# Two attention blocks, gated: projections as two 64-row sums in two PSUM banks, and the maxima shared out anew

## The chip, the cores and the metric

The kernel runs on one core of a Trainium2 chip. The engines of a core work side by side, each in the order of its own instruction list, and wait for each other by semaphores: TensorE (PE; its weight loads are shown as PEld), VectorE (DVE), ScalarE (ACT), GpSimd (POOL), and SyncE (SP), which here only issues DMAs. Matmul results go to PSUM, of which the kernel uses eight banks of 128 x 512 float32. The metric is the device time of one execution in microseconds (us), lower is better, as the median of several runs.

## The reference

Two multi-head attention blocks A and B with weights of their own work on the same input `x` (1 x 2048 x 640), with 32 heads of 20 features each. A gate per token mixes their outputs.

```python
g = _sigmoid((x * gate_w).sum(-1, keepdims=True))
qkv = (x @ wqkv).reshape(B, S, 3, H, Dh)          # H = 32, Dh = 20
scores = jnp.einsum("bhqd,bhkd->bhqk", q, k) * scale
p = _softmax(scores, axis=-1)
o = jnp.einsum("bhqk,bhkd->bhqd", p, v)
a = o.transpose(0, 2, 1, 3).reshape(B, S, D) @ wo     # b likewise
return g * a + (1 - g) * b
```

The softmax is over 2048 keys, for 2048 queries, 32 heads and two blocks. Everything is float32; the kernel holds operands of score and projection matmuls as sums of two float16 parts (`hi` and `lo`).

## The kernel before

**Groups and steps.** The work is cut into 16 groups `g` of four heads (eight per attention block), four query blocks `qb` of 512 queries, and eight steps `i` of 256 keys: 512 steps `G` in all. In each step TensorE makes eight score tiles of 128 keys x 512 queries (`scores`, L632; a head's features fill 64 of the array's 128 rows, so that two heads run at once in the upper and the lower half). ScalarE turns each into exponentials (L635). Two value products (`values`, L650: four heads side by side, 128 rows each, float32) add the step before's exponentials times V into the bank `acc`; a column of ones beside V collects the sum of the exponentials. Behind the last step of a query block `take_acc` divides, on VectorE and GpSimd, and stores.

**Maxima.** The softmax's maximum is found ahead of time, by units that run some 15 steps before the step that needs them. One unit (`max_mm`, L574) makes eight score tiles of 128 queries x 512 keys: four key chunks `ch`, taken in the order 0, 2, 1, 3, times two heads `j`. Each tile is reduced by VectorE to one maximum per query (L585). There is a second form, by key differences: as max(a, b) = b + max(a - b, 0), chunk 0 is multiplied with the difference of the keys of chunks 0 and 1 (tile `kd`), ScalarE takes the relu (L578), and VectorE adds chunk 1 to it and reduces both in one fused operation (L582, followed by a short read of its accumulator). So two reductions on VectorE become one relu on ScalarE and one fused operation. Before the change this is done for head `j == 0` of each pair, and for both heads in the first group.

**Projections.** Q, K and V of the coming group, the rest of Q, and the outputs `o @ wo` are made beside the steps, in blocks of 15 matmuls (9 or 6 for outputs over fewer features) that add up in one bank: five chunks of 128 features times the three products hi x hi, hi x lo, lo x hi. These matmuls use all 128 rows. `mms` (L375) issues them. `project_chunk` makes 512 tokens in three blocks of 176, 168 and 168 columns, and ScalarE copies each out of PSUM with a scale `QKS` (L402); GpSimd splits the chunk into two float16 parts (L404, L405). `project_v` makes 160 columns and ScalarE copies them into V (L530). `out_tiles` makes blocks of 160 or 320 columns; the first job is scaled out by ScalarE (L715), the others are scaled and added by VectorE (L717). The first group's projections run ahead of the steps, in another order, with 512 columns.

**Banks and order.** One of the eight PSUM banks is `acc`; seven are handed out by `take`, which picks the bank that is free earliest by the planner's own clock (`clock`, `free_at`, with costs such as `T_EXP`), and given back by `give` when its reader is through. The planner only chooses banks; the order of work in a step is written out by hand in `STEP`, one line for steps with no, one, or two blocks: `e0`/`e1` is a score tile of the upper or lower half, `m0`/`m1` a tile for the maxima, `V` a value product, and `X` a projection block.

```python
STEP = ("e0 m1 V e1 m0 e0 m1 e1 m0 e0 m1 e1 m0 V e0 m1 e1 m0",
        "X e0 m1 m0 e1 m0 m1 V m1 e0 e1 m0 e1 e0 V m0 e1 e0 m1",
        "X m0 m1 e0 m1 e0 e1 V e1 e0 m1 m0 V e1 m0 m1 m0 e0 e1 X")
```

So in a step with one block, X follows the four scores with which the step before ended, and six scores follow X before the first V. All engines run their lists strictly in this order.

**Queues.** Nearly all DMAs are issued by SP (`nc.sync`), one after the other: the spread of Q and K into the tiles that scores read (`spread`, `rows`, L421 and L423), the key differences (`spread_differences`), maxima, outputs.

Of the kernel before, what the change touches and what calls it, by code (L numbers as in the profile page):

```python
# [11 lines left out]
F32 = mybir.dt.float32  # L12
I32 = mybir.dt.int32
AF = mybir.ActivationFunctionType
# [47 lines left out]
def kernel(  # L62
# [18 lines left out]
    psum = ctx.enter_context(tc.tile_pool(name="psum", bufs=1, space=PSUM))  # L81
# [18 lines left out]
    acc = psum.tile([P, QB], F32, name="acc")  # L100
# [59 lines left out]
    def scales(maxima, n, then):  # L160
# [5 lines left out]
        nc.tensor.transpose(pt[:n, :P], maxima[:, :n], ident)  # L166
# [3 lines left out]
        nc.vector.tensor_reduce(e[:n, 0:1], pt[:n, :P], axis=AX.X, op=OP.max)  # L170
# [11 lines left out]
        for k in range(2):  # L182
            nc.tensor.matmul(pb[:, k * n:(k + 1) * n], ones[:n, :], dg[:n, k, :n], start=True, stop=True)  # L183
        yield
        both = wts.tile([P, 10], F32, name="both", tag="scb", bufs=2)
        nc.vector.tensor_copy(both[:, :2 * n], pb[:, :2 * n])
# [181 lines left out]
    def mms(i, out_ap, pairs, cost):  # L368

        if now[0] >= 0:  # L370
            tick_block(len(pairs) * cost * T_SCORE, free_at[i])
        for k, (a, b) in enumerate(pairs):
            if now[0] < 0:
                tick_block(cost * T_SCORE, free_at[i])
            nc.tensor.matmul(out_ap, a, b, start=(k == 0), stop=(k == len(pairs) - 1))  # L375
            if now[0] < 0:
                yield
# [6 lines left out]
    def project_chunk(w, hi, lo, ch):  # L384
# [9 lines left out]
        if now[0] >= 0:  # L394
            f = work.tile([P, QB], F32, name="fs")
            for k in range(3):
                if k:
                    yield
                m = slice(PARTS[k], PARTS[k + 1])
                i, pt = take()  # L400
                yield from mms(i, pt[:, m], pairs(slice(t0 + m.start, t0 + m.stop)), 0.34)
                nc.scalar.activation(f[:, m], pt[:, m], AF.Copy, scale=QKS)  # L402
                give(i, spend("act", 0.25, clock["done"]))
# [115 lines left out]
    def project_v(gg, j):  # L519
# [3 lines left out]
        for u in range(2):  # L523
            if u and now[0] >= 0:
                yield
            n = slice((j + u) * P, (j + u + 1) * P)
            i, pt = take()
            yield from mms(i, pt[:, :w], [(a[:, c, n], b[:, c, :w]) for c in range(NC) for a, b in
                                          ((xh, wh), (xh, wl), (xl, wh))], 0.33)
            nc.scalar.activation(V[gg % 2][:, j + u, :, 0:DH], pt[:, :160].rearrange("p (h d) -> p h d", h=2 * GH),  # L530
                                 AF.Copy, scale=QKS)
            give(i, spend("act", 0.25, clock["done"]))
            v_done.add((gg, j + u))
            if gg == 0:
                nc.scalar.activation(gates[:, 0, j + u:j + u + 1], pt[:, 160:161], AF.Exp, scale=inv_g)
# [16 lines left out]
    relus, relu_at = {}, {}  # L552

    def max_parts(g, qb):
        m = mparts[g, qb] = wts.tile([P, 2, 2, 4, 4], F32, name="mpart", tag="mpart", bufs=2)
        nc.gpsimd.memset(m[:, :, 0:1 if g else 2, :, 0] if g or qb else m, LOW)

    def max_mm(u, ch, heads=(0, 1)):
# [9 lines left out]
        for j in heads:  # L568
            two = u < NS or ch < 2 and (j == 0 or g == 0)
# [4 lines left out]
            nc.tensor.matmul(pt, QT[g % 2][r, pair, q0:q0 + P], k, start=True, stop=True)  # L574
            m = mparts[g, qb][:, pair, j, t, ch:ch + 1]
            if two and ch % 2 == 0:
                relus[u, j] = start.tile([P, QB], F32, name="rl0", bufs=4) if u < NS else work.tile([P, QB], F32, name="rl", bufs=2)
                nc.scalar.activation(relus[u, j], pt, AF.Relu)  # L578
                back = relu_at[u, j] = spend("act", T_EXP, ready)
            elif two:  # L580
                rl = relus.pop((u, j))
                nc.vector.tensor_tensor_reduce(rl, pt, rl, 1.0, LOW, OP.add, OP.max, m)  # L582
                back = spend("dve", T_MAX, max(ready, relu_at.pop((u, j))))
            else:
                nc.vector.tensor_reduce(m, pt, axis=AX.X, op=OP.max)  # L585
# [38 lines left out]
    def scores(G, kk, pair, heads=(0, 1)):  # L624
# [3 lines left out]
        for j in heads:  # L628
# [3 lines left out]
            nc.tensor.matmul(et, KT[g % 2][r, pair, kt * P:(kt + 1) * P],  # L632
                             QT[g % 2][r, pair, qb * QB:(qb + 1) * QB], start=True, stop=True)
            pt = pp.tile([P, QB], F32, name="pt")
            nc.scalar.activation(pt, et, AF.Exp, scale=factor(g // 4))  # L635
# [49 lines left out]
    def out_tiles(job, t, state):  # L685
# [491 lines left out]
```

## Time and profile before

| | us |
|---|---|
| median of 3 runs (2834.72 to 2834.99) | 2834.94 |
| span of the profiled execution | 2832.8 |
| TensorE busy | 2773.1 |
| ScalarE busy | 2529.7 |
| VectorE busy | 2443.8 |
| GpSimd busy | 671.8 |
| share of projections (L375) in the chain that ended last | 20% |

The profiled execution's span is 2.1 us under the median of the runs. In rows of instruction groups, the line of the kernel and the engine come first, then what is written and read, the shapes, and the count; behind the bar stand the group's busy time in us, the mean ns of one, and how long the engine stood idle before them, with what ended that. In a timeline a row has its start and length in us; neighbours of one kind are merged (x2, x6). A matmul's row is longer than the time it holds the array, since they are pipelined: the distance of two starts tells what one costs. The mean granted clock of TensorE was 0.996.

### The profile page before, as it was taken

How to read it: one execution, taken by the hardware profiler on the slowest of the kernel's cores; microseconds unless marked ns; L12 is line 12 of the kernel's file. 1: busy time of each engine (PE TensorE's matmuls, PEld its weight loads, DVE VectorE, ACT ScalarE, POOL GpSimd, SP SyncE). 2: the span in 40 equal slices, each digit the busy share in tenths (PEclk: the TensorE clock that was granted, in tenths of full speed). 3: DMA queues.
4: the chain of work that ended last, by engine and by line, in shares of the span. 5: the costliest groups of instructions: out<-in, count | busy, mean ns of one | idle time of the engine just before them, and what ended most of it. 6: DMA issues, size and time to landing. Idle time of an engine off the chain costs nothing.

```text
span 2832.8 us, 62443 instructions
## 1 busy us (share of the span) xinstructions
PE 2773.1 (98%) x23362; PEld 970.8 (34%) x23362; DVE 2443.8 (86%) x4763; ACT 2529.7 (89%) x5122; POOL 671.8 (24%) x914
## 2 busy tenths in 40 slices
PE   6999999999999999999999999999999999999998
PEld 3533223342323323343233333334333333332222
DVE  6688999879999898988989888887888989989982
ACT  3799999989999999989999999998899999888887
POOL 5312113231221212233431111222112233120011
PEclk9999999999999999999999999999999999999999
DMA  4110101001020101202021020211202112122222
GB/s 135 35 45 7 39 6 42 16 16 29 13 52 16 37 11 27 47 13 50 17 56 44 14 60 16 48 37 24 49 15 61 38 38 70 55 71 60 63 60 74
DMA packets 167170, 113.71 MB, mean 40 GB/s; under 512 B 102224, under 2 KB 140808, under 8 KB 166864
## 3 DMA queue, kind: packets, MB, share of 16 engines
q1 hardware_dynamic: 164320, 108.09, 15.6%
q8 instruction: 183, 3.00, 0.4%
q0 software_dynamic: 1600, 0.96, 0.2%
q14 instruction: 123, 1.01, 0.1%
q10 hardware_dynamic: 944, 0.66, 0.1%
HBM read 48.89 MB, written 26.61 MB: 27 GB/s over the span
## 4 chain that ended last, share of the span: by engine, by line
PE 91%; DVE 5%; ACT 1%; DMA 1%; POOL 1%; issue 1%; SPq 0%; POOLq 0%; DVEq 0%; ACTq 0%
PE acc L650 34%; PE bank L375 20%; PE bank L632 19%; PE bank L574 17%; DVE mpart L585 3%; ACT pt L635 1%; DVE rl L582 1%; DMA xs<-in_A_x_dram 0%; ACT rl L578 0%; DMA wv<-in_A_wqkv_dram 0%; DVE ot L736 0%; PE bank L813 0%; PE bank L183 0%; PE bank L862 0%; DVE wmax L227 0%
## 5 line engine op out<-in xcount | busy, mean ns | idle before, releaser
L635 ACT ACTIVATE pt<-bank 128x512 f32<-128x512 f32 x4096 | 2157.5, 614 | 155.0 <-PE bank L632 75.1
L585 DVE TENSOR_REDUCE mpart<-bank 128x1 f32<-128x512 f32 x2976 | 1867.8, 681 | 264.3 <-PE bank L574 167.1
L650 PE MATMUL acc<-pt,v 128*21 128x512 f32 x8192 | 1082.0, 600 | 3.4 <-DVE ot L736 3.1
L632 PE MATMUL bank<-qt,kt 64*128 64x512 f16 x4096 | 1056.3, 380 | 11.9 <-ACT pt L635 4.5
L574 PE MATMUL bank<-kt,qt 60*128 60x512 f16 x3536 | 1013.0, 380 | 4.0 <-DVE mpart L585 0.7
L574 PEld LDWEIGHTS <-qt 60*128 60x128 f16 x4096 | 235.4, 94 | 686.6 <-issue 629.0
L632 PEld LDWEIGHTS <-kt 64*128 64x128 f16 x4096 | 248.1, 94 | 456.7 <-issue 322.8
L582 DVE CUSTOM_DVE_ANT_0 rl<-bank,rl 128x512 f32<-128x512 f32 x560 | 377.5, 678 | 20.5 <-ACT rl L578 8.2
L578 ACT ACTIVATE rl<-bank 128x512 f32<-128x512 f32 x560 | 329.8, 595 | 14.6 <-PE bank L574 12.3
L744 POOL TENSOR_TENSOR ot<-ot,sq 128x512 f32<-128x512 f32 x63 | 66.0, 1047 | 993.0 <-DVE sq L741 993.0
L650 PEld LDWEIGHTS acc<-pt,v 128*21 128x21 f32 x8192 | 143.0, 99 | 434.6 <-issue 421.5
L375 PE MATMUL bank<-xx,wbh 128*128 128x168 f16 (+2 forms) x2240 | 280.1, 244 | 3.2 <-ACT xx L866 1.9
L375 PE MATMUL bank<-xx,wbl 128*128 128x168 f16 (+2 forms) x1120 | 252.8, 243 | 0.0
L375 PEld LDWEIGHTS <-wbh 128*128 128x128 f16 x2240 | 183.6, 98 | 86.8 <-issue 79.8
L574 PE MATMUL bank<-kd,qt 60*128 60x512 f16 x560 | 203.6, 381 | 1.7 <-DMA kd<-dd 1.2
L375 PE MATMUL bank<-wvh,xx 128*128 128x160 f16 (+1 forms) x1280 | 155.4, 234 | 0.5 <-ACT pt L635 0.3
L375 PE MATMUL bank<-woh,o_in 128*128 128x160 f16 (+1 forms) x960 | 155.7, 256 | 0.0
L375 PEld LDWEIGHTS <-xx 128*128 128x128 f16 x1920 | 131.6, 97 | 52.7 <-issue 49.4
L404 POOL CAST cq<-fs 128x512 f16<-128x512 f32 x60 | 36.6, 609 | 446.0 <-ACT fs L402 444.0
L375 PE MATMUL bank<-wvl,xx 128*128 128x160 f16 (+1 forms) x640 | 137.3, 231 | 0.6 <-POOL wvl L315 0.6
L375 PEld LDWEIGHTS <-o_in 128*128 128x128 f16 (+1 forms) x1440 | 104.0, 97 | 75.3 <-issue 62.2
L402 ACT ACTIVATE fs<-bank 128x168 f32<-128x168 f32 (+1 forms) x216 | 67.5, 313 | 56.6 <-PE bank L375 40.0
(131 smaller groups left out, 1305.2 us busy)
## 6 DMA issues: line engine op xcount, KB each, us to landing
y_scr<-y_out SPq DMA_DIRECT2D x32, 320.0 KB
kt<-cq SPq DMA_DIRECT2D x120, 80.0 KB
o_scr<-on SPq DMA_DIRECT2D x240, 40.0 KB
kt<-cq SPq DMA_DIRECT2D x136, 40.0 KB
xs<-in_A_x_dram SPq DMA_DIRECT2D x8, 640.0 KB
o_in<-o_scr SPq DMA_DIRECT2D x32, 160.0 KB
y_out<-y_scr SPq DMA_DIRECT2D x16, 320.0 KB
xx<-y_scr SPq DMA_DIRECT2D x16, 320.0 KB
```

The costliest lines, as they stand in the source:

```text
L375: nc.tensor.matmul(out_ap, a, b, start=(k == 0), stop=(k == len(pairs) - 1))
L402: nc.scalar.activation(f[:, m], pt[:, m], AF.Copy, scale=QKS)
L404: nc.gpsimd.tensor_copy(hi, f)
L574: nc.tensor.matmul(pt, QT[g % 2][r, pair, q0:q0 + P], k, start=True, stop=True)
L578: nc.scalar.activation(relus[u, j], pt, AF.Relu)
L582: nc.vector.tensor_tensor_reduce(rl, pt, rl, 1.0, LOW, OP.add, OP.max, m)
L585: nc.vector.tensor_reduce(m, pt, axis=AX.X, op=OP.max)
L632: nc.tensor.matmul(et, KT[g % 2][r, pair, kt * P:(kt + 1) * P], QT[g % 2][r, pair, qb * QB:(qb + 1) * QB], start=True, stop=True)
L635: nc.scalar.activation(pt, et, AF.Exp, scale=factor(g // 4))
L650: nc.tensor.matmul(acc[32 * h:32 * h + VW, :], V[(g // 2) % 2][:, kt, (g % 2) * GH + h, :], ptiles.pop((G, kk, h)), start=(kt == 0), stop= ...
L744: nc.gpsimd.tensor_tensor(t3, t3, sq.unsqueeze(2).to_broadcast([P, 16, 32]), op=OP.mult)
```

## The change

Three things are changed.

**The form of a projection block.** Each matmul over 128 rows becomes two over 64 rows each, which run at once in the two halves of the array, like scores. Each half adds up in a bank of its own; the two banks are neighbours, and one VectorE instruction (`tensor_reduce` over the two) adds them and writes the sum. ScalarE has no part in it any more. What it scaled is now scaled elsewhere: V isn't scaled (its ones become `1 / QKS`), chunks of Q and K are scaled on GpSimd before the split, and outputs are scaled and added on GpSimd. The projections ahead of the steps stay as they were. For the steps the seven banks are one tile (`store`), and `apart` lifts waits between readers and writers of different banks, over the last 24 readers; the last few instructions of the kernel (`alone=False`) keep theirs.

**The maxima.** In every second unit (`u % 2`) both heads use the key differences, instead of one head.

**What follows from that.** The key differences are spread for both heads in every group: four more DMAs on SP for each of 15 groups.

```diff
-    psum = ctx.enter_context(tc.tile_pool(name="psum", bufs=1, space=PSUM))
+    psum_acc = ctx.enter_context(tc.tile_pool(name="psum_acc", bufs=1, space=PSUM))
+    psum_start = ExitStack()
+    psum = psum_start.enter_context(tc.tile_pool(name="psum", bufs=1, space=PSUM))
...
-    acc = psum.tile([P, QB], F32, name="acc")
+    acc = psum_acc.tile([P, QB], F32, name="acc")
     banks = [psum.tile([P, QB], F32, name=f"bank{i}") for i in range(NB)]
...
+    def take_two():
+
+        i = min((k for k in range(NB - 1) if k not in held and k + 1 not in held),
+                key=lambda k: (max(max(free_at[k:k + 2]), clock["pe"]), abs(free_at[k] - free_at[k + 1])))
+        held.update((i, i + 1))
+        return (i, i + 1), store[0][:, i:i + 2]
+
+    store, last_read = [], {}
+
+    fresh, recent = set(), []
+
+    def apart(ins, keep):
+
+        for r, engine in recent:
+            if r not in keep and engine != ins.engine:
+                tc.declare_no_dep(ins, r, reason="a reader of another bank")
+
+    def on_bank(out, ins, alone=True):
+
+        if store:
+            i = out.offset // QB
+            if alone:
+                apart(ins.ins, last_read.get(i, []))
+            fresh.add(i)
+        return ins
+
+    def matmul(out, a, b, start=True, stop=True, alone=True):
+        return on_bank(out, nc.tensor.matmul(out, a, b, start=start, stop=stop), alone)
+
+    def transpose(out, a, alone=True):
+        return on_bank(out, nc.tensor.transpose(out, a, ident), alone)
+
+    def read(banks_read, ins, keep=(), alone=True):
+
+        name = ins.ins.name
+        if store:
+            for i in banks_read:
+                if i in fresh:
+                    fresh.discard(i)
+                    last_read[i] = []
+                last_read[i].append(name)
+            if alone:
+                apart(ins.ins, keep)
+            recent.append((name, ins.ins.engine))
+            del recent[:-24]
+        return name
...
     def mms(i, out_ap, pairs, cost):
 
-        if now[0] >= 0:
-            tick_block(len(pairs) * cost * T_SCORE, free_at[i])
         for k, (a, b) in enumerate(pairs):
-            if now[0] < 0:
-                tick_block(cost * T_SCORE, free_at[i])
-            nc.tensor.matmul(out_ap, a, b, start=(k == 0), stop=(k == len(pairs) - 1))
-            if now[0] < 0:
-                yield
+            tick_block(cost * T_SCORE, free_at[i])
+            matmul(out_ap, a, b, start=(k == 0), stop=(k == len(pairs) - 1))
+            yield
+
+    def halves_of(pairs, w):
+
+        ik, two = take_two()
+        t = max(clock["pe"], max(rows_free), max(free_at[i] for i in ik))
+        parts = [[(a[p0:min(p0 + 64, a.shape[0])], b[p0:min(p0 + 64, a.shape[0])]) for a, b in pairs if a.shape[0] > p0]
+                 for p0 in (0, 64)]
+        for k in range(len(parts[0])):
+            for j in range(2):
+                if k < len(parts[j]):
+                    matmul(two[:, j, :w], *parts[j][k], start=(k == 0), stop=(k == len(parts[j]) - 1))
+        rows_free[:] = [t + len(parts[0]) * w / QB * T_SCORE] * 2
+        clock["pe"], clock["done"] = t, rows_free[0] + T_READY - T_SCORE
+        return ik, two[:, :, :w]
+
+    def summed_halves(ik, two, w, scale, to, shape=lambda x: x):
+
+        read(ik, nc.vector.tensor_reduce(to, shape(two.rearrange("p b n -> p n b")), axis=AX.X, op=OP.add))
+        t = spend("dve", 0.06 + 2 * w / 960, clock["done"])
+        for i in ik:
+            give(i, t)
...
-                m = slice(PARTS[k], PARTS[k + 1])
-                i, pt = take()
-                yield from mms(i, pt[:, m], pairs(slice(t0 + m.start, t0 + m.stop)), 0.34)
-                nc.scalar.activation(f[:, m], pt[:, m], AF.Copy, scale=QKS)
-                give(i, spend("act", 0.25, clock["done"]))
+                w = PARTS[k + 1] - PARTS[k]
+                ik, two = halves_of(pairs(slice(t0 + PARTS[k], t0 + PARTS[k + 1])), w)
+                summed_halves(ik, two, w, QKS, f[:, PARTS[k]:PARTS[k + 1]], lambda x: x)
+            nc.gpsimd.tensor_scalar(f, f, QKS, None, op0=OP.mult)
             nc.gpsimd.tensor_copy(hi, f)
...
-        for j in range(2 if g == 0 else 1):
+        for j in range(2):
...
-            i, pt = take()
-            yield from mms(i, pt[:, :w], [(a[:, c, n], b[:, c, :w]) for c in range(NC) for a, b in
-                                          ((xh, wh), (xh, wl), (xl, wh))], 0.33)
-            nc.scalar.activation(V[gg % 2][:, j + u, :, 0:DH], pt[:, :160].rearrange("p (h d) -> p h d", h=2 * GH),
-                                 AF.Copy, scale=QKS)
-            give(i, spend("act", 0.25, clock["done"]))
+            pairs = [(a[:, c, n], b[:, c, :w]) for c in range(NC) for a, b in ((xh, wh), (xh, wl), (xl, wh))]
+            to = V[gg % 2][:, j + u, :, 0:DH]
+            if now[0] >= 0:
+                ik, two = halves_of(pairs, w)
+                summed_halves(ik, two, w, QKS, to, lambda x: x.rearrange("p (h d) b -> p h d b", h=2 * GH))
+            else:
+                i, pt = take()
+                yield from mms(i, pt[:, :w], pairs, 0.33)
+                nc.scalar.activation(to, pt[:, :160].rearrange("p (h d) -> p h d", h=2 * GH), AF.Copy, scale=1.0)
+                give(i, spend("act", 0.25, clock["done"]))
+                if gg == 0:
+                    nc.scalar.activation(gates[:, 0, j + u:j + u + 1], pt[:, 160:161], AF.Exp, scale=inv_g)
...
-        nc.gpsimd.memset(m[:, :, 0:1 if g else 2, :, 0] if g or qb else m, LOW)
+        nc.gpsimd.memset(m[:, :, :, :, 0] if g or qb else m, LOW)
...
-            two = u < NS or ch < 2 and (j == 0 or g == 0)
+            two = u < NS or ch < 2 and (j == 0 or g == 0 or u % 2)
...
-            nc.tensor.matmul(pt, QT[g % 2][r, pair, q0:q0 + P], k, start=True, stop=True)
+            matmul(pt, QT[g % 2][r, pair, q0:q0 + P], k, start=True, stop=True)
...
-                nc.scalar.activation(relus[u, j], pt, AF.Relu)
+                relu_by[u, j] = read([i], nc.scalar.activation(relus[u, j], pt, AF.Relu), keep=added)
...
-                nc.vector.tensor_tensor_reduce(rl, pt, rl, 1.0, LOW, OP.add, OP.max, m)
+                added.append(read([i], nc.vector.tensor_tensor_reduce(rl, pt, rl, 1.0, LOW, OP.add, OP.max, m),
+                                  keep=[relu_by[u, j]]))
+                del added[:-4]
...
-                i, pt = take()
-                yield from mms(i, pt[:, :width], [(o[:p, a, c - c0], w[:p, c, n])
-                                                  for c in range(c0, c1) for p in (P if c < full else 48,)
-                                                  for a, w in ((0, wh), (0, wl), (1, wh))], width / QB)
+                ik, two = halves_of([(o[:p, a, c - c0], w[:p, c, n]) for c in range(c0, c1)
+                                     for p in (P if c < full else 48,) for a, w in ((0, wh), (0, wl), (1, wh))], width)
                 f = f_o[z][:, t:t + 1]
+                part = y[:, n] if first else work.tile([P, QB], F32, name="fs")[:, :width]
+                summed_halves(ik, two, width, 1.0, part)
                 if first:
-                    nc.scalar.activation(y[:, n], pt[:, :width], AF.Copy, scale=f)
+                    nc.gpsimd.tensor_scalar(part, part, f, None, op0=OP.mult)
                 else:
-                    nc.vector.scalar_tensor_tensor(y[:, n], pt[:, :width], f, y[:, n], op0=OP.mult, op1=OP.add)
-                give(i, spend("act" if first else "dve", 0.08 + width / 900, clock["done"]))
+                    nc.gpsimd.tensor_scalar(part, part, f, None, op0=OP.mult)
+                    nc.gpsimd.tensor_tensor(y[:, n], y[:, n], part, op=OP.add)
...
-        nc.gpsimd.memset(V[i][:, :, :, DH:VW], 1.0)
+        nc.gpsimd.memset(V[i][:, :, :, DH:VW], 1.0 / QKS)
...
+    psum_start.close()
+    psum = ctx.enter_context(tc.tile_pool(name="psum_steps", bufs=1, space=PSUM))
+    store.append(psum.tile([P, NB, QB], F32, name="bank"))
+    banks[:] = [store[0][:, i] for i in range(NB)]
```

More of the change, by code (lines that the diff above doesn't have):

```diff
@@ L182, in scales @@
         for k in range(2):
-            nc.tensor.matmul(pb[:, k * n:(k + 1) * n], ones[:n, :], dg[:n, k, :n], start=True, stop=True)
+            matmul(pb[:, k * n:(k + 1) * n], ones[:n, :], dg[:n, k, :n], start=True, stop=True)
         yield
         both = wts.tile([P, 10], F32, name="both", tag="scb", bufs=2)
-        nc.vector.tensor_copy(both[:, :2 * n], pb[:, :2 * n])
+        read([i], nc.vector.tensor_copy(both[:, :2 * n], pb[:, :2 * n]))
         give(i, spend("dve", 0.2, clock["done"]))
@@ L776, in take_last @@
         for t in range(4):
[L777 removed]
+            matmul(pt[:, 4 * t:4 * t + 4], ot[:, t * P:(t + 1) * P], one, start=True, stop=True, alone=False)
         rc = work.tile([P, 16], F32, name="sq", bufs=2)
[L779 removed]
+        read([i], nc.vector.reciprocal(rc, pt[:, :16]), alone=False)
         give(i, spend("dve", 0.3))
         i, pt = take()
[L782 removed]
+        transpose(pt[:16, :P], rc, alone=False)
         rt = wts.tile([16, P], F32, name="rt", tag="rt", bufs=1)
[L784 removed]
+        read([i], nc.scalar.activation(rt, pt[:16, :P], AF.Copy), alone=False)
         give(i, spend("act", 0.3))
@@ L787, in take_last @@
         for t in range(4):
-            nc.tensor.matmul(pt[:, t * P:(t + 1) * P], picks[0].rearrange("p k e -> p (k e)")[:, t * P:(t + 1) * P], rt,
-                             start=True, stop=True)
+            matmul(pt[:, t * P:(t + 1) * P], picks[0].rearrange("p k e -> p (k e)")[:, t * P:(t + 1) * P], rt,
+                   start=True, stop=True, alone=False)
         o = work.tile([P, 2, QB], F16, name="on", bufs=2)
```

28 lines of the change are left out of this document (11 added, 17 removed).

## The prediction, made before the change was run

> **What bounds the kernel now.** I read the page first: busy time by engine, then the chain of waits.
>
> ```profile
> span 2832.8 us, 62443 instructions
> ...
> PE 2773.1 (98%) x23362; PEld 970.8 (34%) x23362; DVE 2443.8 (86%) x4763; ACT 2529.7 (89%) x5122; POOL 671.8 (24%) x914
> ...
> PE 91%; DVE 5%; ACT 1%; DMA 1%; POOL 1%; issue 1%; SPq 0%; POOLq 0%; DVEq 0%; ACTq 0%
> PE acc L650 34%; PE bank L375 20%; PE bank L632 19%; PE bank L574 17%; DVE mpart L585 3%; ACT pt L635 1%; DVE rl L582 1%; DMA xs<-in_A_x_dram 0%; ACT rl L578 0%; DMA wv<-in_A_wqkv_dram 0%; DVE ot L736 0%; PE bank L813 0%; PE bank L183 0%; PE bank L862 0%; DVE wmax L227 0%
> ```
>
> TensorE is the bound, and a fifth of the chain is the projections (L375), which the change rewrites. But VectorE and ScalarE are close behind, so I looked by stretch: one without projections, then one step with a projection block.
>
> ```profile
> 1000.00:1030.00 30.00, 29.19 (x206) 7.07 (x206) 29.00 (x56) 28.65 (x58) 2.81 (x7) 1.00 0.09 19
> 1830.43:1835.61 5.18, 5.18 (x52) 1.84 (x55) 4.38 (x9) 4.95 (x11) 1.09 (x1) 1.00 0.27 53
> ```
>
> The columns are PE, PEld, DVE, ACT, POOL. Without a block all three engines are full; with one, TensorE alone sets the pace. What a cheaper block is worth is therefore read from the second kind, in the timeline of one step:
>
> ```profile
> 1831.35 0.39 PE L574 MATMUL bank<-kt,qt 60*128 60x512 f16 x1
> ...
> 1831.81 3.04 ACT L635 ACTIVATE pt<-bank 128x512 f32<-128x512 f32 x6 [0.20 <-PE bank L632]
> ...
> 1833.10 0.39 PE L574 MATMUL bank<-kt,qt 60*128 60x512 f16 x1
> ...
> 1833.33 0.38 PE L574 MATMUL bank<-kt,qt 60*128 60x512 f16 x1
> 1833.52 1.29 DVE L585 TENSOR_REDUCE mpart<-bank 128x1 f32<-128x512 f32 x2 [0.37 <-PE bank L632]
> ...
> 1833.64 0.24 PE L375 MATMUL bank<-woh,o_in 128*128 128x160 f16 x1
> ...
> 1834.40 0.75 SPq L423 DMA_DIRECT2D qt<-rk  x1
> ...
> 1834.62 0.23 PE L375 MATMUL bank<-woh,o_in 128*128 128x160 f16 x1
> ...
> 1834.78 0.39 PE L632 MATMUL bank<-qt,kt 64*128 64x512 f16 x1
> ...
> 1834.89 0.39 ACT L715 ACTIVATE y_out<-bank,f_o 128x160 f32<-128x160 f32 x1
> ...
> 1835.20 0.60 ACT L635 ACTIVATE pt<-bank 128x512 f32<-128x512 f32 x1
> 1835.23 0.38 PE L574 MATMUL bank<-kt,qt 60*128 60x512 f16 x2
> 1835.24 2.48 DVE L585 TENSOR_REDUCE mpart<-bank 128x1 f32<-128x512 f32 x4 [0.43 <-PE bank L574]
> ...
> 1835.54 1.06 PE L650 MATMUL acc<-pt,v 128*21 128x512 f32 x8
> ```
>
> The reader is to see two things. First, the seams. Score pairs start 0.22 us apart (three of them from 1834.78 to 1835.23). The last pair before the block starts at 1833.33, so the array is free at 1833.55, yet the block starts at 1833.64: 0.09 lost. Its 15 matmuls start 0.07 apart (0.98 over 14), so it is through at 1834.69, and the next score starts at 1834.78: 0.09 again. Second, the banks. The six exponentials run every (3.04 - 0.60) / 5 = 0.49 us, so the fourth ends at 1833.88. At 1833.55 the fourth to sixth exponential and both reductions are unfinished: five of the seven banks are taken.
>
> **Part 1: the seams go.** Scores already use half the array's rows, two at a time; a block in the same form needs no change of form on either side. The 15 pairs should stream as 15 matmuls do, 0.07 each, if loads and matmuls are issued fast enough. Per block: -0.09 - 0.09 = -0.18. How many blocks: the first operand runs twice per block of 15, so by x / 10:
>
> ```profile
> L375 PE MATMUL bank<-xx,wbh 128*128 128x168 f16 x1440 | 171.0, 238 | 0.0
> ...
> L375 PE MATMUL bank<-wvh,xx 128*128 128x160 f16 x1120 | 136.8, 234 | 0.5 <-ACT pt L635 0.3
> ...
> L375 PE MATMUL bank<-xx,wbh 128*128 128x176 f16 x720 | 88.8, 240 | 1.1 <-ACT rl L578 0.9 <-DVE mpart L585 0.2
> L375 PE MATMUL bank<-woh,o_in 128*128 128x160 f16 x640 | 76.5, 234 | 0.0
> ...
> L375 PE MATMUL bank<-woh,o_in 128*128 128x320 f16 x256 | 63.1, 302 | 0.0
> ```
>
> 144 + 112 + 72 + 64 = 392, and of the 320-wide, two jobs of 32 blocks (6 and 2 such matmuls in each: 192 + 64 = 256). 32 of these 64 lie among scores and maxima, 32 at the very end. So 424 blocks in the body. Bounds of the gain: 0.18, or nothing if the pairs stream slower. I take 0.18, because this burst shows eight weight loads starting within 0.14 - 0.10 = 0.04 us of a wait's end (one takes about 0.10):
>
> ```profile
> 164.29 0.14 PEld L650 LDWEIGHTS acc<-pt,v 128*21 128x21 f32 x8 [1.51 <-DVE ot L736]
> ```
>
> **Part 2: two banks at the block's start.** At 1833.55 exactly two of seven banks are free, and the block now wants two that are neighbours. By counting places, two free banks are neighbours in 6 of 21 cases, three contain a neighbouring pair in 25 of 35. The third comes free with the fourth exponential at 1833.88 (0.33 later), the next with the first reduction at 1833.52 + 0.68 = 1834.20 (0.65 later). So the wait is 0 in 0.29 of the blocks, 0.33 in 0.43, about 0.65 in the rest: 0.33. The planner's pair search prefers the earliest pair, so I shade this to 0.26. Ends: 0 and 0.65. Everything behind the block on TensorE waits with it, then ScalarE and VectorE, which have drained meanwhile and gain nothing.
>
> **Part 3: two banks after the block's end.** Behind X, the step's order has six scores before the next V. Five banks are left for them; the sixth must take one of the block's own. None of the first five is released in time: the first exponential ends at 1835.80, over 1.0 us after its score. So the sixth waits for VectorE's sum. The reduction has this price from rows of its kind:
>
> ```profile
> L585 DVE TENSOR_REDUCE mpart<-bank 128x1 f32<-128x512 f32 x2976 | 1867.8, 681 | 264.3 <-PE bank L574 167.1 <-PE bank L632 84.7
> ...
> L402 ACT ACTIVATE fs<-bank 128x168 f32<-128x168 f32 x144 | 44.7, 310 | 31.0 <-PE bank L375 24.1
> ...
> L592 DVE TENSOR_REDUCE mneg<-mpart 128x16 f32<-128x64 f32 x64 | 14.0, 218 | 5.9 <-DVE mpart L585 0.5
> ```
>
> (681 - 218) / (512 - 64) = 1.03 ns per element and 152 ns fixed: 2 x 168 elements take 0.50 us, 2 x 320 take 0.81. An evacuation starts 0.27 after the last matmul's start (1834.89 - 1834.62). So the banks come back 0.77 after that start, and the sixth score, with the seam gone, wants one at 0.07 + 0.22 + 0.22 = 0.51. Wait: 0.26. Ends: 0.07 if the sum took only ScalarE's 0.31, and 0.60 if two banks cost twice per element (0.15 + 0.69 = 0.84). Today's block holds one bank, and six scores fit in six.
>
> **Part 4: who does the rest.** The evacuations change engines:
>
> ```profile
> L582 DVE CUSTOM_DVE_ANT_0 rl<-bank,rl 128x512 f32<-128x512 f32 x560 | 377.5, 678 | 20.5 <-ACT rl L578 8.2 <-PE bank L574 7.7 <-ACT v L530 1.0
> ...
> L530 ACT ACTIVATE v<-bank 128x160 f32<-128x160 f32 x128 | 39.1, 306 | 13.6 <-PE bank L375 9.7
> ...
> L715 ACT ACTIVATE y_out<-bank,f_o 128x160 f32<-128x160 f32 x64 | 25.2, 393 | 7.5 <-PE bank L375 6.1
> ...
> L402 ACT ACTIVATE fs<-bank 128x176 f32<-128x176 f32 x72 | 22.8, 317 | 25.6 <-PE bank L375 15.9 <-issue 6.5 <-POOL cq L405 1.9
> ...
> L717 DVE SCALAR_TENSOR_TENSOR y_out<-bank,f_o,y_out 128x320 f32<-128x320 f32 x32 | 17.5, 548 | 8.0 <-PE bank L375 4.7 <-issue 2.5 <-ACT pt L635 0.6
> ```
>
> VectorE gains 456 sums, 246 us by the formula above, and loses 64 scalings of 0.55 (35 us) and, on the odd units behind the first group (512 - 32, halved: 240), two reductions for one fused operation each. Reductions run every (2.48 - 0.68) / 3 = 0.60 and the fused one costs about 0.68: 240 x 0.52 = 125 us less. Net +86 on 2443.8. ScalarE loses 44.7 + 22.8 + 25.2 + 112 x 0.306 = 127 us of evacuations and gains 240 relus at its 0.49 pace, 118 us. Neither grows past the bound in steps with a block; without one, VectorE's relief and ScalarE's load cancel. I cost it at nothing, with +-29 if half of the 240 units fall where one of them is not covered (0.24 each). GpSimd takes the scalings:
>
> ```profile
> L305 POOL TENSOR_SCALAR wstage<-wstage,r_qk 128x400 f32<-128x400 f32 x15 | 19.3, 1284 | 0.0
> ...
> L305 POOL TENSOR_SCALAR wstage<-wstage,r_o 128x800 f32<-128x800 f32 x8 | 18.3, 2284 | 0.3
> ```
>
> 2.5 ns per element and 0.28 fixed: 72 x 1.56 + 64 x 0.68 + 64 x 1.08 = 225 us, and some 42 for the adds, on an engine that is 76% idle; uncovered it would delay a chunk's spread by 1.6 us, steps ahead of its use. Sixty more key-difference DMAs (15 groups, 4 each, 0.75 of SP's queue by the row above) delay what follows them on SP by 3 us per group: the same cover, 45 us without it. The seven banks become one tile, and hand-written lines lift the waits between different banks for the last 24 readers: nothing, if they do; a wait that stayed would be for another bank's reduction, 0.6. In the last stage they are kept, over a dozen instructions; and the first score of the steps waits once for all old banks. Both under 2 us, left out.
>
> **Sum.** Per block -0.18 + 0.26 + 0.26 = +0.34, times 424: +144. The last 32 blocks stand among few scores; they only lose seams (0.18 each): -6. Span 2832.8 + 138 = 2971; the runs' median lies 2.1 above the span: 2973.
>
> **Rivals.**
> The waits vanish: neighbours are always free, and the sixth score finds a bank. Then 456 x -0.18 = -82: 2753. For it: 98% busy TensorE is the bound. Against: five banks taken at the block's start, in the rows above.
>
> Gains and waits cancel, if neighbours are always free and the sum takes 0.42 (wait 0.18): 2835 less the late 6.
>
> VectorE and ScalarE become the bound: even units keep six reductions (3.6), one fused (0.68) and the sum (0.50) on VectorE, 4.8 before any transposes, against today's 5.18; odd units put ten activations (4.9) on ScalarE. The seams then return nothing, and half of the odd units cost 0.24 more: 2835 + 29 = 2864. It decides as soon as the two engines' work per step passes TensorE's. The 29.00 and 28.65 of 30 above speak for it; but in the step with a block VectorE is busy 4.38 of 5.18.
>
> Issue is the limit: the densest stream that lasts is a load and a matmul each 0.07. If that is the sequencer's and not the array's, 15 pairs take 2.1 us: 424 x (1.05 + 0.34) = +589: 3424. Against it: the burst of eight loads. The Trainium skill (TensorE: Matmul & The Clock Gate, "Wait — 56ns, not 53.3ns?") says that with hardware decode off each matmul costs the sequencer about 62 ns, an estimate of 30 x 0.062 = 1.9 us per block. By that rule the block would nearly double; the burst does not bear it out, but it could have been queued ahead.
>
> The Trainium skill (TensorEngine Tiling (Array Packing), "Gotcha 1: PSUM Pressure") has different row tiles in different banks, and more pressure on PSUM for it. It prices nothing; the bank counts here are where this case would show it.
>
> **Chances.** Bank waits outweigh the seams: 0.62, its own range 2870 to 3080 (waits of 0 and 0.26 give 424 x 0.08 = +34; waits of 0.5 and 0.26 give +246). Waits vanish: 0.17. Cancel: 0.07. Engines bound: 0.10. Issue: 0.04. Within 0.2% is what a measurement here cannot tell from no change. Faster 0.17, same 0.07, slower 0.76. The range takes in most of the gain's side and the long waits: 2800 to 3085.
>
> **What would show it.** Right: no gap at the end of the score pairs before a block, 15 pairs in 1.05 us, but waits of TensorE on bank releases at the block's first matmul and at the sixth score behind it, about 0.26 each, the second released by the new sum; VectorE and ScalarE busy shares lower. Wrong: a block step at 5.0 us; pair starts over 0.08 apart; a sum well under 0.4 us; VectorE on most of the chain.

## The result and the profile after

The changed kernel takes 3150.31 us (median of 4 runs, 3148.94 to 3151.62), against 2834.97 before (4 runs, 2834.72 to 2835.01). The ratio is 1.1113, with a 95% interval of 1.1097 to 1.1129: slower by 315 us, where 138 were predicted. The page of the changed kernel has the span, the engines, and the chain by engine:

```profile
span 3147.3 us, 75939 instructions
...
PE 2908.7 (92%) x29626; PEld 1050.9 (33%) x29626; DVE 2525.1 (80%) x5155; ACT 2531.2 (80%) x4970; POOL 945.5 (30%) x1178
...
PE 64%; ACT 16%; DVE 8%; issue 6%; POOL 4%; DMA 1%; SPq 0%; ACTq 0%; DVEq 0%; POOLq 0%
```

TensorE held 91% of the chain and now holds 64%; ScalarE has gone from 1% to 16%. All three engines have a lower busy share than before (98, 86 and 89%). So no engine has become the bound: the engines wait for each other. What TensorE waits for stands in its rows of the view of waits (us in total, times, longest):

```profile
PE bank L157 <- DVE mpart L656: 82.8, 130, 2.6
PE bank L157 <- ACT pt L706: 78.9, 220, 0.8
```

The largest wait of this kind in the steps of the kernel before, with the waits at the very start left aside, was

```profile
PE bank L632 <- ACT pt L635: 4.5, 16, 0.5
```

That is some 160 us of waits against almost nothing; some 38 us of the first row are stops behind a fill on GpSimd, which is told below. The rows don't hold all waits for banks, because a matmul's row is drawn longer than it holds the array (0.38 us for a score, where score pairs start 0.22 apart). So the first 0.16 us of a wait are drawn as busy, and a wait of one half of the array is covered by the row of the other half. For such waits one reads starts, not idle time. The timeline around one block (start, duration, engine and line; in brackets the idle time before it):

```profile
2007.10 0.39 PE L157 MATMUL bank<-kt,qt 60*128 60x512 f16 x1
...
2007.33 0.38 PE L157 MATMUL bank<-kt,qt 60*128 60x512 f16 x1
2007.53 1.29 DVE L656 TENSOR_REDUCE mpart<-bank 128x1 f32<-128x512 f32 x2 [0.45 <-PE bank L157]
...
2007.93 0.24 PE L157 MATMUL bank<-woh,o_in 64*128 64x160 f16 x2 [0.22 <-ACT pt L706]
...
2008.00 0.24 PE L157 MATMUL bank<-wol,o_in 64*128 64x160 f16 x2
...
2008.89 0.25 PE L157 MATMUL bank<-woh,o_in 64*128 64x160 f16 x2
...
2008.96 0.38 PE L157 MATMUL bank<-qt,kt 64*128 64x512 f16 x1
2008.98 0.57 PE L157 MATMUL bank<-kd,qt 60*128 60x512 f16 x2
...
2009.18 0.49 DVE L440 TENSOR_REDUCE y_out<-bank 128x160 f32<-128x320 f32 x1 [0.37 <-PE bank L157]
...
2009.20 0.38 PE L157 MATMUL bank<-qt,kt 64*128 64x512 f16 x1
...
2009.40 0.70 PE L157 MATMUL bank<-kt,qt 60*128 60x512 f16 x2
...
2010.03 0.14 PEld L721 LDWEIGHTS acc<-pt,v 128*21 128x21 f32 x8 [0.73 <-issue]
```

The last score pair starts at 2007.33, so the array is free at 2007.55. The block starts at 2007.93, when an exponential of ScalarE has given a bank back: 0.38 lost. Its 15 pairs start 0.07 apart and the next score stands at 2008.96, 1.03 behind the block's start, without a seam. Of the six scores behind it the fifth starts at 2009.40 and the sixth at 2009.40 + 0.70 - 0.38 = 2009.72, not at once with its partner: the sum on VectorE ended at 2009.18 + 0.49 = 2009.67, and 0.05 later the bank was in use again. 0.30 lost. Both waits of the prediction are there, each longer than its 0.26 here.

A third is not in the prediction. The timeline of another place, and the granted clock of TensorE around it (in the second view the columns are PE, PEld, DVE, ACT and POOL, then the clock, the DMA share and GB/s):

```profile
1785.59 1.49 POOL L468 TENSOR_SCALAR fs<-fs 128x512 f32<-128x512 f32 x1 [0.25 <-DVE fs L440]
...
1786.85 0.39 PE L157 MATMUL bank<-qt,kt 64*128 64x512 f16 x2
...
1787.14 0.61 POOL L469 CAST cq<-fs 128x512 f16<-128x512 f32 x1
...
1787.84 1.15 POOL L470 TENSOR_TENSOR cq<-fs,cq 128x512 f16<-128x512 f32 x1
...
1788.93 0.12 POOL L625 MEMSET mpart<- 128x16 f32 x1
1789.09 1.29 DVE L656 TENSOR_REDUCE mpart<-bank 128x1 f32<-128x512 f32 x2 [3.59 <-POOL mpart L625]
...
1789.83 0.39 PE L157 MATMUL bank<-kt,qt 60*128 60x512 f16 x2 [2.60 <-DVE mpart L656]
```

```profile
1788.00:1790.00 2.00, 0.17 (x2) 0.09 (x1) 0.91 (x2) 0.36 (x1) 1.06 (x2) 1.00 0.24 51
1790.00:1794.00 4.00, 4.00 (x32) 1.33 (x32) 3.00 (x7) 1.20 (x3) 0.00 (x0) 0.57 0.33 76
1794.00:1800.00 6.00, 6.00 (x83) 2.60 (x78) 4.25 (x9) 4.32 (x9) 1.78 (x2) 1.00 0.23 39
```

The tile of partial maxima, one for the eight units of a group and query block, is filled with a low value by GpSimd (L625, 0.12 us). The fill stands in GpSimd's queue behind the scaling and the split of a chunk (L468 to L470); the scaling is new there. VectorE's first reduction into the tile waits 3.59 us for it, TensorE stands still for 2.60, and when it starts again its granted clock is 0.57 in the mean of four microseconds.

### The profile page after: what moved, and what is told of

Same layout as the page of the kernel before. It is cut to its first block, busy times and chain, and to the rows that moved or that the text cites. A ratio compares the mean times of both kernels' runs of the same rounds, so it can differ in the third digit from the quotient of the medians.

```text
span 3147.3 us, 75939 instructions
## 1 busy us (share of the span) xinstructions
PE 2908.7 (92%) x29626; PEld 1050.9 (33%) x29626; DVE 2525.1 (80%) x5155; ACT 2531.2 (80%) x4970; POOL 945.5 (30%) x1178
## 4 chain that ended last, share of the span: by engine, by line
PE 64%; ACT 16%; DVE 8%; issue 6%; POOL 4%; DMA 1%; SPq 0%; ACTq 0%; DVEq 0%; POOLq 0%
PE bank L157 41%; PE acc L721 22%; ACT pt L706 14%; DVE mpart L656 4%; ACT rl L647 2%; DVE rl L651 1%; POOL fs L468 1%; DVE fs L440 1%; DVE ot L807 1%; POOL fs L788 1%; DVE ob L818 0%; DMA xs<-in_A_x_dram 0%; POOL ot L815 0%; DMA wv<-in_A_wqkv_dram 0%; POOL cq L469 0%
## 5 line engine op out<-in xcount | busy, mean ns | idle before, releaser
L656 DVE TENSOR_REDUCE mpart<-bank 128x1 f32<-128x512 f32 x2496 | 1592.6, 682 | 240.1 <-PE bank L157 166.6
L651 DVE CUSTOM_DVE_ANT_0 rl<-bank,rl 128x512 f32<-128x512 f32 x800 | 531.6, 683 | 121.8 <-PE bank L157 78.5
L157 PE MATMUL bank<-xx,wbh 64*128 64x168 f16 (+2 forms) x4400 | 303.2, 240 | 54.9 <-ACT pt L706 30.6
L157 PEld LDWEIGHTS <-wbh 64*128 64x128 f16 (+1 forms) x4400 | 238.1, 96 | 132.5 <-issue 102.8
L440 DVE TENSOR_REDUCE fs<-bank 128x168 f32<-128x336 f32 (+2 forms) x280 | 162.7, 582 | 139.7 <-PE bank L157 125.1
L468 POOL TENSOR_SCALAR fs<-fs 128x512 f32<-128x512 f32 x72 | 107.2, 1489 | 543.6 <-DVE fs L440 523.4
L157 PE MATMUL bank<-xx,wbl 64*128 64x168 f16 (+2 forms) x2200 | 262.3, 239 | 0.0
L157 PE MATMUL bank<-wvh,xx 64*128 64x160 f16 (+1 forms) x2400 | 163.0, 230 | 31.0 <-ACT pt L706 17.1
L157 PE MATMUL bank<-woh,o_in 64*128 64x160 f16 (+2 forms) x1856 | 160.1, 252 | 27.3 <-ACT pt L706 16.8
L157 PEld LDWEIGHTS <-xx 64*128 64x128 f16 (+1 forms) x3600 | 144.9, 94 | 76.1 <-issue 58.0
L157 PEld LDWEIGHTS <-wbl 64*128 64x128 f16 (+1 forms) x2200 | 147.4, 95 | 4.3 <-issue 0.8
```

The source lines that it names most:

```text
L157: return on_bank(out, nc.tensor.matmul(out, a, b, start=start, stop=stop), alone)
L440: read(ik, nc.vector.tensor_reduce(to, shape(two.rearrange("p b n -> p n b")), axis=AX.X, op=OP.add))
L468: nc.gpsimd.tensor_scalar(f, f, QKS, None, op0=OP.mult)
L651: added.append(read([i], nc.vector.tensor_tensor_reduce(rl, pt, rl, 1.0, LOW, OP.add, OP.max, m), keep=[relu_by[u, j]]))
L656: read([i], nc.vector.tensor_reduce(m, pt, axis=AX.X, op=OP.max))
```

## The experiments

Every time is a median of 4 runs, its ratio against the kernel before on the same chip. Steps were also compared by kind, each from its first value product to that of the next step: 107 have no projection block in this stretch, 344 have one, 60 have two. Blocks were compared where they are full (15 matmuls, or 15 pairs) and have six scores between them and the next V; every kernel has 293 of these.

### Which half of the change costs what

The form of the projections alone (the changed kernel with the old share of maxima, key differences and fill), and the new share of maxima alone, put into the kernel before:

```diff
-        for j in range(2):
+        for j in range(2 if g == 0 else 1):
...
-        nc.gpsimd.memset(m[:, :, :, :, 0] if g or qb else m, LOW)
+        nc.gpsimd.memset(m[:, :, 0:1 if g else 2, :, 0] if g or qb else m, LOW)
...
-            two = u < NS or ch < 2 and (j == 0 or g == 0 or u % 2)
+            two = u < NS or ch < 2 and (j == 0 or g == 0)
```

(The second kernel has the same three lines the other way round.)

> The changed kernel with the maxima shared out as before (one head by key differences). If the waits on PSUM banks around each projection block make the loss, they stay: 3110 to 3150 us, the 25 us that steps without a block lost coming back at most. If the new loads of VectorE and ScalarE make it, most of it moves: either far above 3150 (VectorE was in need of the relief) or below 2950.

> The kernel before with only the new share of the maxima. Banks: 2835 to 2870 us, ScalarE's ten activations in every second step costing up to 0.24 us in steps without a block. Load: above 2950.

Form alone: 3060.98 us, ratio 1.08 (1.0782 to 1.0818). Share alone: 2869.84, 1.0124 (1.0107 to 1.0141). So the form costs 226 us. The first expectation was too high, because the share isn't free (the second is met, at its upper end): alone it costs 35 us, and on top of the form 3150 - 3061 = 89.

The form's 226 us stand beside this: in the 293 blocks, the mean time from the last score before the block to the next V was 0.313 + 1.178 + 0.787 = 2.278 us before (to the block's start, to the next score, to V) and is 0.427 + 1.257 + 1.136 = 2.820 in the form alone. That is 0.54 more per block, where 0.34 was predicted; times 424, as an estimate for all blocks, it makes 230.

### The fill

The fill moved to VectorE, in the changed kernel and in the share alone:

```diff
-        nc.gpsimd.memset(m[:, :, :, :, 0] if g or qb else m, LOW)
+        (nc.vector if g or qb else nc.gpsimd).memset(m[:, :, :, :, 0] if g or qb else m, LOW)
```

> The changed kernel with the fill of the maxima tile on VectorE, not GpSimd. VectorE waited 54.7 us for GpSimd's fill in the changed kernel and not at all before. If that wait is on the path: 3095 to 3115 us. If it is only idle time that another wait would take: 3140 to 3155.

> The kernel before with the new share of the maxima and the fill of the maxima tile on VectorE. With GpSimd's fill it took 2870 us, VectorE waiting 27.9 us for it. If that wait is on the path: 2843 to 2855, the rest being ScalarE's ten activations in steps without a block. If not: 2865 to 2870.

Changed kernel: 3087.37 (1.089, 1.0872 to 1.0908), 63 us less. Share alone: 2852.94 (1.0066, 1.0049 to 1.0083), 17 less. These are the rows of the view of waits that went away, first of the changed kernel, then of the share alone:

```profile
DVE mpart L656 <- POOL mpart L625: 54.7, 25, 3.6
```

```profile
DVE mpart L585 <- POOL mpart L556: 27.9, 15, 3.0
```

54.7 us of waits, and 63 gained, more than expected: part of the cost is the clock. TensorE's own waits for the reductions, 82.8 us in the changed kernel, are 38 us shorter with the fill on VectorE:

```profile
PE bank L157 <- DVE mpart L656: 44.6, 101, 0.7
```

The lost share of TensorE's granted clock, times the time that it lasted, adds up to 40.2 us in the changed kernel, 12.6 before, 12.8 in the form alone and 16.7 with the fill on VectorE, which is 23.5 less. Together these are 62 of the 63 us.

Leaving aside the first 150 and the last 20 us, the clock of the changed kernel falls in 12 places, 1.7 or 3.4 us lost in each. All 12 are at one of the 13 fill waits over 2 us, where TensorE stood still for 1.76 to 2.60; at the 12 shorter ones (up to 1.85, TensorE still for 1.11 or less) it doesn't fall. With the fill on VectorE it falls nowhere in that time. This gives no fixed limit: in the kernel with the sum in two operations (below) the clock falls at a stop of 1.62 us (2644.0), and at one of 2.76 (1543.2) it doesn't. The Trainium skill (TensorE: Matmul & The Clock Gate, "What's actually happening") lets the array's clock drop to half after an idle window of about 3.4 us. The trace agrees with the fall, 0.57 in the slice above, and not with the length, since these stops were 2.60 or less.

### The seams

To see what the two 64-row halves save, the block was put back to full-row matmuls, taking the two banks in turn; the sum stays (the planner's times for the block, left out here, change with it). First in the changed kernel, later in a kernel with freely chosen banks (the last of the next part).

```diff
...
-        parts = [[(a[p0:min(p0 + 64, a.shape[0])], b[p0:min(p0 + 64, a.shape[0])]) for a, b in pairs if a.shape[0] > p0]
-                 for p0 in (0, 64)]
-        for k in range(len(parts[0])):
-            for j in range(2):
-                if k < len(parts[j]):
-                    matmul(two[:, j, :w], *parts[j][k], start=(k == 0), stop=(k == len(parts[j]) - 1))
...
+        for k, (a, b) in enumerate(pairs):
+            matmul(two[:, (len(pairs) - k) % 2, :w], a, b, start=(k < 2), stop=(k >= len(pairs) - 2))
...
```

> The changed kernel with 128-row matmuls that alternate between the two banks, summed as in the change: two banks and the sum without the 64-row form. If the form saves its seams of 0.18 us per block and the banks cost the rest: 3150 + 0.18 x 390 = 3220 us. If the 64-row form itself is slow (issue, weight loads): under 3150.

> The kernel of the last run (any two banks, ScalarE copies one, maxima as before) with 128-row matmuls that alternate between the two banks. With the old choice of banks this form cost only 4 us more than the 64-row form. If the saved seams were hidden behind the waits for banks, they show now, at least the one ahead of each block: 0.09 x 390 = 35 us more, 2915 us, up to 2950 for both. If 64-row pairs save nothing in themselves: 2880.

With the neighbouring banks: 3154.51 (1.1126, 1.1108 to 1.1145), 4 us over the changed kernel, not 70; the intervals of the two overlap. With free choice: 2904.61 (1.0253, 1.0236 to 1.027) against 2881.55, 23 us, between the two cases that were expected. The prediction had 0.18 x 424 = 76 us of gain. Where the block starts when a bank is released, an array that is free 0.09 earlier waits 0.09 longer. With the full rows the mean time from the last score over the block to the next score is 0.581 + 1.270, against 0.446 + 1.265, so 0.140 longer; but from there to V it is 1.006 in place of 1.135, so 0.129 shorter. My reading of this is that the sum is nearer to its end when the sixth score comes. The expectation of 70 us missed what it should have taken from the prediction's own second part.

### Which banks, and for how long

Three steps, each on top of the one before. First, the sum in two operations, so that the second bank is released earlier (VectorE copies it out, then adds the first). Then any two free banks in place of neighbours. Then ScalarE does the copy.

```diff
-        read(ik, nc.vector.tensor_reduce(to, shape(two.rearrange("p b n -> p n b")), axis=AX.X, op=OP.add))
...
+        read(ik[1:], nc.vector.tensor_copy(part, two[1]))
+        give(ik[1], spend("dve", 0.06 + w / 960, clock["done"]))
+        read(ik[:1], nc.vector.tensor_tensor(to, view(two[0]), view(part), op=OP.add))
+        give(ik[0], spend("dve", 0.06 + w / 960))
```

```diff
-        i = min((k for k in range(NB - 1) if k not in held and k + 1 not in held),
-                key=lambda k: (max(max(free_at[k:k + 2]), clock["pe"]), abs(free_at[k] - free_at[k + 1])))
+        i, k = sorted((k for k in range(NB) if k not in held), key=lambda k: free_at[k])[:2]
```

```diff
-        read(ik[1:], nc.vector.tensor_copy(part, two[1]))
+        copied = read(ik[1:], nc.scalar.activation(part, two[1], AF.Copy), keep=halved)
...
```

> The changed kernel with the sum in two VectorE operations: a copy of the second bank to SBUF, then an add of the first. The second bank comes back after one of some 0.32 us instead of 0.50. If the sixth score behind a block waits for a bank of the block, it starts some 0.18 us earlier at each of about 390 blocks: 3080 us. If VectorE's load is the limit, the added 0.15 us per block make it slower: up to 3210.

> The two-operation sum (3115 us) with any two free banks for a block, neighbours or not. If the wait for neighbours is what holds a block's start, some 0.4 us of about 0.5 go at each of 370 blocks: 2965 us. If the count of free banks holds it: 3100 to 3120.

> As the run before, but the copy of the second bank to SBUF is ScalarE's, and VectorE only adds. Banks: the second bank is back at the same time, so within 20 us of the run before. If VectorE's load is the limit: 40 us or more under it. If ScalarE's is: over it.

Two operations: 3114.85 (1.0987, 1.0969 to 1.1006). The sixth score came earlier as expected (0.964 from the next score to V, 0.171 less), but from the last score over the block to the next score it took 0.05 longer, and the time fell by 35 us, not 70. Any two banks: 2986.38 (1.0534, 1.0516 to 1.0552), another 128 us less; the mean time from the last score to the block fell from 0.548 to 0.226, where 0.22 is a score pair without any wait. ScalarE's copy: 2973.91 (1.0486, 1.0469 to 1.0504), 12 us less, as expected if neither VectorE's load nor ScalarE's is the limit.

Then the old share of maxima on top, the best form of the change found:

> As the run before, with the maxima shared out as in the kernel before. The share of the maxima cost 89 us with the two-bank blocks and 35 alone: 35 to 89 us under the run before, 2880 us by the banks' theory. If a free choice of banks gains nothing: over 3000.

2881.55 (1.0167, 1.015 to 1.0184). A block in its timeline:

```profile
1861.33 0.38 PE L157 MATMUL bank<-kt,qt 60*128 60x512 f16 x1
...
1861.55 0.23 PE L157 MATMUL bank<-woh,o_in 64*128 64x160 f16 x2
...
1862.58 0.38 PE L157 MATMUL bank<-qt,kt 64*128 64x512 f16 x1
...
1862.79 0.30 ACT L442 ACTIVATE hs<-bank 128x160 f32<-128x160 f32 x1
...
1863.02 0.50 PE L157 MATMUL bank<-kt,qt 60*128 60x512 f16 x2
...
1863.12 0.33 DVE L445 TENSOR_TENSOR y_out<-bank,hs 128x160 f32<-128x160 f32 x1 [0.31 <-ACT hs L442]
```

The block starts 0.22 behind the last pair, as the prediction's first part had it: no gap on either side. ScalarE's copy is through at 1863.09, and the sixth score starts at 1863.02 + 0.50 - 0.38 = 1863.14, where its pair stood at 1863.02. TensorE is busy for 97% again:

```profile
PE 2792.3 (97%) x29626; PEld 1055.1 (37%) x29626; DVE 2529.8 (88%) x5155; ACT 2510.2 (87%) x5186; POOL 945.1 (33%) x1178
```

It still loses 46 us to the kernel before: 2 in the steps without a block, 21 in those with one, 23 in those with two. From the last score to the next V one of the 293 blocks takes 0.222 + 1.130 + 0.957 = 2.309, still more than the 2.278 of before: 0.14 are gained up to the next score, but behind it, where the sixth score waits for its bank, 0.17 are lost.

### One bank fewer in the kernel before

To price a bank by itself, the kernel before runs its steps with six banks instead of seven; nothing else changes.

```diff
     start_stack.close()
+    held.add(NB - 1)
```

> The kernel before with six banks instead of seven from the first step on. By the count of banks a block still finds its one bank (five of six are taken), and the sixth score behind it wants the block's bank at 0.60 us after the last matmul's start, when ScalarE's copy gives it back at 0.63: 2840 to 2880 us. If it is the number of banks left for scores that made the changed kernel slow, rather than two at once and a longer sum: above 2950.

2984.08 (1.0528, 1.0511 to 1.0546): 149 us for one bank. That is the second case of the expectation; the first, which had counted only places where the order of a step needs the seventh bank, is far off. The growth is 39 us in steps without a block, 86 in those with one and 23 in those with two. So the count of free places was the wrong model. What fits, though no run tests it by itself, is that VectorE and ScalarE also need scores that are done ahead, so that they never wait, and that a bank less takes that lead everywhere: by the views of waits VectorE's reductions (L585) waited 376 us for scores, against 252 before, and ScalarE's exponentials (L635) 240, against 133. Their busy shares are lower too (86 and 89% before):

```profile
PE 2900.2 (97%) x23362; PEld 993.3 (33%) x23362; DVE 2460.2 (82%) x4763; ACT 2542.9 (85%) x5122; POOL 671.5 (23%) x914
```

## Why the prediction was right or wrong

The direction was right, and so was the main mechanism: the waits for banks outweigh the seams. Three terms of the sum failed: both waits were too short, and the new share of the maxima, put at nothing, had a cost. The time was 177 us too low, outside the range. In us:

| step of the prediction | predicted | measured | from |
|---|---|---|---|
| blocks: seams and both waits | +138 | +226 | form alone against before |
| share of maxima and its fill | 0 | +89 | changed kernel against form alone |
| sum | +138 | +315 | |

**Part 1, the seams**, has the right picture and the wrong worth. The blocks stream as predicted: 15 pairs in 1.03 us, no gap at the end. But 0.09 on each side was booked as gain beside a wait that follows in the same place, and a gain ahead of a wait for a release is no gain. Against full rows in the same two banks, the form is worth 4 us here and 23 where the banks are free, not 76.

**Part 2, two neighbouring banks**, is one of the two steps that failed by size. Without any wait, the way from the last score through the block to the next score takes 1.29 us (0.217, and 1.07 as the mean of the three widths). It takes 1.684 in the form alone and 1.711 in the changed kernel, in the 293 blocks: a wait of 0.40 and 0.42, where the count of places gave 0.33 and I shaded it to 0.26 because the planner looks for the earliest pair. The planner did not help. It plans with estimated times, and in about 80 of the blocks of the changed kernel the first half starts and the second waits over 0.4 us for its bank. The step taken apart shows the cause: on top of the sum in two operations, free choice of banks gives 128 us back.

**Part 3, the sixth score**, failed by size as well. From the block's next score to V the form alone takes 1.136, against 0.756 without a wait (the median before): 0.38, and the same in the changed kernel, predicted 0.26. The price of the sum was right, by two of its rows, count, busy time and mean:

```profile
L440 DVE TENSOR_REDUCE fs<-bank 128x168 f32<-128x336 f32 x144 | 72.8, 505 | 52.2 <-PE bank L157 49.9
...
L440 DVE TENSOR_REDUCE fs<-bank 128x320 f32<-128x640 f32 x64 | 52.4, 822 | 39.8 <-PE bank L157 37.4 <-POOL xx L789 2.2
```

0.505 and 0.822 us, predicted 0.50 and 0.81. What was left out are three smaller things: from the sum's end to the matmul it is 0.05; in 36 of the 293 blocks of the changed kernel VectorE had other work first, in 19 of them a reduction, and the sum started 0.70 behind the last matmul on average, not at 0.27; and blocks of 320 columns, which are not among the 293, hold their banks 0.32 longer. In the median the wait is 0.34 (1.093 to V).

Per block the form alone now adds up like this. Without any wait, the way from the last score to V takes 1.29 + 0.76, some 2.04, which is 0.24 under the 2.278 of before (predicted: 0.18 under). The waits add 0.40 and 0.38 (predicted: 0.26 each). That is +0.54, not +0.34, and over all blocks 226 - 138 = 88 us.

**Part 4, who does the rest**, was costed at nothing, and 89 us are there. The loads themselves were priced well: VectorE is busy for 81 us more (predicted 86), ScalarE for 2 more (9 less), GpSimd for 274 more (267). The cover named was an idle GpSimd. It is idle, 30% busy, but it works in order: a fill of 0.12 us waits behind up to 3.25 us of scaling and splitting (1.49 + 0.61 + 1.15 above). Before, the fill touched only slots that no plain reduction of VectorE writes; the new share makes it cover both heads, and the first plain reduction that writes a filled slot (of the second head, in an even unit) waits for it. The prediction priced the length of what moved to GpSimd, but not what was queued behind it and who waited for that. Of the 89 us 63 are the fill, by the run with the fill on VectorE. The rest, 26, is near the 18 us that the share without this wait costs alone, 10 of them in steps without a block; for these the prediction had named up to 29 us and left them out of its sum.

**The rivals.** "The waits vanish" and "cancel" fall with the waits in the timeline; even with freely chosen banks and the old share the change loses 46 us. "VectorE and ScalarE become the bound" falls by the page: both are at 80%; what is left of it are the 18 us of the share. "Issue is the limit" falls by the block's 1.03 us: 30 loads and 30 matmuls, 0.034 us for each matmul. The 62 ns per matmul that the Trainium skill (TensorE: Matmul & The Clock Gate, "Wait — 56ns, not 53.3ns?") gives for hardware decode off are not what these matmuls took; no run here shows whether it was off. The Trainium skill's sentence on pressure on PSUM (TensorEngine Tiling (Array Packing), "Gotcha 1: PSUM Pressure") is borne out: one bank fewer cost 149 us, the neighbours 128.

**What stays open.** The steps with two blocks in the best form still lose 23 us, and I have not found by which wait. Whether the lines that lift waits between different banks leave some behind had no run of its own; in the steps without a block the best form takes only 2 us more than the kernel before, so there it is little. A rearranged order of the step (five scores behind the block, for instance), or sums that are put into another place, was not tried. No kernel here beats the one before.

## What to carry to other kernels

Count banks as time, not as places: an output that holds two banks until another engine has read both is paid for by every producer that ran ahead through them, and choosing any two free banks was worth more here (128 us) than one instruction that reads neighbours. Do not add a gain and a wait that follow each other at one place; take the later end. When work moves to an idle engine, list what is queued behind it there, small fills too, and who waits for them.

## What the runs showed of the hardware

- Two 64-row matmuls at once, each with its own weight load, start 0.07 us apart per pair, as one 128-row matmul with its load does (N = 160): 15 pairs in 1.03 us.
- A bank released by VectorE was written by TensorE again 0.05 us after the reader's end (2009.67 to 2009.72).
- After stops of 1.76 to 2.60 us TensorE's granted clock fell (a mean of 0.57 over four microseconds in the slice shown), 1.7 or 3.4 us lost each time; the twelve falls of the changed kernel lost some 25 us in all. At one such stop, of 2.39 us (282.7), it didn't fall.
